# The sign of a weight's low word: one 32-bit VectorE instruction with two operands, or one 16-bit instruction with one

## The chip, the cores and the metric

The kernel runs on one core of one Trainium2 chip. The metric is the device time of one execution in microseconds (us). A core has five engines that work side by side, each through its own queue in order: TensorE (PE; its weight loads are PEld in the profile), VectorE (DVE), ScalarE (ACT), GpSimd (POOL) and SyncE (SP), which issues the transfers here.

## The reference

Three layers follow one another, all in float32:

```python
scores = scale * q @ k.T                     # 4 batches, 8 heads, 576 positions, 64 per head
attn   = (scores * Dmat) @ v                 # Dmat[i, j] = gamma[h] ** (i - j) for i >= j, else 0
x = attn, heads side by side                 # 2304 tokens x 512
h = x @ w_in                                 # 512 x 2048
y = (h * tanh(log1p(exp(h)))) @ w_out        # 2048 x 512
# then a routed layer: every token goes to one of 8 experts by sorted logits,
# 288 tokens each, out = relu(y @ w1[e]) @ w2[e]
```

The change lies in how `w_in` and `w_out` are prepared for the second layer.

## The kernel before

Matrix products are made from two words of each number: a high word (`hi`, the rounded value) and a low word (`lo`, the rest). A product is then three matmuls: high by high, low by high, high by low. So each weight tile of 128 x 512 has to be split once into `hi` and `lo`. There are 32 such tiles, 16 of `w_in` (`winh`, `winl`) and 16 of `w_out` (`woh`, `wol`). The host hands them over as 64-bit integers, so no plain float view of them is loaded: it is the kernel that turns the 64-bit element into a float32 one. `raw` is the loaded tile; `w0` is the low and `w1` the high 32-bit word of each element.

The class `convert` does that for one tile, in seven instructions:

- `c` (L160, ScalarE): copies `w1` with a scale into the work tile `t` (named y or spare in the profile).
- `x1` (L163, ScalarE): takes the 16-bit upper half of `w0` (`top`), and writes its top bits, as an integer, over `w0`, as 32-bit elements.
- `x` (L167, VectorE): takes the sign bit of `w1` and ors it into `w0`.
- `a` (L172, VectorE): shifts `t` left by three bits and ors `w0` into it. `t` is then the float32 weight. After it the next tile's transfer into the free buffer is issued (`fetch`, L141).
- `h` (L178, ScalarE): writes the high word. `l` (L181, GpSimd, in a few early cases VectorE): subtracts it from `t`, which gives the low word.

The second layer is laid out as a list of steps (`steps`, from `plan`). A step takes one block of 256 tokens and one of 16 slices of the hidden size: `ff_h` (L323, TensorE, 12 matmuls), the activation (`ff_a1` with L332 to L340, `ff_a2` with the reciprocal at L345, `ff_b1` L350, `ff_b2` L358, `ff_b3` L364 and L365), and three steps later `ff_y` (L417, six matmuls). The loop at L538 writes each engine's queue by hand. As long as there are weights left to convert, nearly every step (`CONV`) also converts one tile, and the attention of later blocks is spread over the steps by tables (`EARLY`, `MID`, `FOUR`).

In a step that converts, the queues hold, in this order:

- VectorE: `x`, `a`, L350 of the step before, L340, L365 of two steps before, L345, L358 of the step before.
- ScalarE: `x1` and `c` (both issued at the end of the step before), L332, L333, L334, L364 of two steps before, `h`.
- GpSimd: `l` of the step before, then the attention's multiplications (L232, L237) where there are any.

Four conversions come before the loop. The last of the 32 ends near 136 us; from then on the steps hold no conversion, and the rest of the time goes to the remaining steps of the second layer and to the routed layer.

Of the kernel before, what the change touches and what calls it, by code (L numbers as in the profile page):

```python
# [13 lines left out]
U16 = mybir.dt.uint16  # L14
I64 = mybir.dt.int64
AF = mybir.ActivationFunctionType
ALU = mybir.AluOpType
# [64 lines left out]
def first_part(ctx, tc, att, att_ht, att_hn, dtab, qtab, ktab, stab, wi, wo, wgb, ydram, L, constants, cst, begin, grid):  # L82
    nc = tc.nc
# [47 lines left out]
    raws = []  # L131
# [3 lines left out]
    done = [0]  # L135
# [7 lines left out]
    class convert:  # L143
# [3 lines left out]
        def __init__(self):  # L147
            _, self.hi, self.lo = parts[done[0]]
            w = raws[done[0]].bitcast(U32).rearrange("p (n two) -> p n two", two=2)
            self.w0, self.w1 = w[:, :, 0], w[:, :, 1]  # L150
            self.top = raws[done[0]].bitcast(U16).rearrange("p (n four) -> p n four", four=4)[:, :, 1]
            self.i = done[0]
            done[0] += 1

# [5 lines left out]
            nc.scalar.activation(self.t, self.w1.bitcast(F32), AF.Copy, scale=2.0 ** -112)  # L160

        def x1(self):
            nc.scalar.activation(self.w0, self.top, AF.Copy, scale=2.0 ** -13, bias=-0.4999)  # L163

        def x(self):
            w0 = self.w0
            nc.vector.scalar_tensor_tensor(w0, self.w1, 0x80000000, w0, op0=ALU.bitwise_and,  # L167
                                           op1=ALU.bitwise_or)

        def a(self):  # L170
            t = self.t.bitcast(U32)
# [364 lines left out]
    for x in slots.get(-1, []):  # L536
        x()
    for i in range(len(steps) + YL):  # L538
# [15 lines left out]
        if new:  # L554
            n, f = steps[i]
            alone = bool(now or old)
            eng = nc.vector if alone else nc.gpsimd
            if not alone:
                for x in slots.get(i, []):
                    x()  # L560
            if i and steps[i - 1] in inv:
                ff_b1(*steps[i - 1], nc.vector)
            ff_a1(n, f, i, alone)
            if i > 1:
                ff_b3(*steps[i - 2], eng)
            if now:
                now.h()
            if alone:
                for x in slots.get(i, []):
                    x()  # L570
                ff_h(*steps[i + 1], i + 1)
            while behind:
                behind.pop()()
            ff_a2(n, f)
            if i:
                ff_b2(*steps[i - 1])
            if eng is not nc.vector:
                ff_b1(n, f, nc.vector if i == len(steps) - 1 else eng)
# [979 lines left out]
```

## Time and profile before

| | |
|---|---|
| median of 3 runs | 824.83 us (824.33 to 826.1) |
| time of the profiled execution | 824.72 us |
| its span | 822.9 us |
| busy over the span: PE, DVE, ACT, POOL | 769.8, 532.7, 434.0, 472.4 us |
| instructions at the changed lines | 32 at L163, 32 at L167 |
| busy time of L167 | 24.2 us, 758 ns each |
| busy time of L163 | 21.3 us, 667 ns each |

The span runs from the first to the last recorded instruction; the execution's time is 1.8 us longer. Busy time is the time in which an engine worked on some instruction. Instructions of one engine overlap a little at their ends, so the distance from one start to the next is shorter than the duration where nothing has to be waited for. The chain of waits follows the work that ended last back to what released it. A row of a timeline gives the start, the duration, the engine, the line, the operation, the tile written and read, and in brackets the idle time before it and what ended it.

### The profile page before, as it was taken

Reading aid. Unit: us, or ns where it says so; the run is one execution under the profiler, and the core shown is the slowest. Engines: PE = TensorE matmul, PEld = TensorE weight load, DVE = VectorE, ACT = ScalarE, POOL = GpSimd, SP = SyncE. Lnnn points to the kernel's source line nnn. Section 1 sums busy time; section 2 is a strip of 40 time slices with the busy share of each in tenths; the row PEclk is TensorE's granted clock in tenths of the full one; section 3 lists DMA queues with packets and bytes.
Section 4 is the critical chain, followed back from the end, with each engine's and each line's share of the span. In section 5 each row is a group of like instructions: output and inputs, shape, how many; then the busy total and the mean of one; then the engine's idle time right before and its main releaser. Section 6 shows DMA issues by size and latency. Waiting matters only on the chain.

```text
span 822.9 us, 16272 instructions
## 1 busy us (share of the span) xinstructions
PE 769.8 (94%) x6151; PEld 704.5 (86%) x6151; DVE 532.7 (65%) x1262; ACT 434.0 (53%) x943; POOL 472.4 (57%) x539
## 2 busy tenths in 40 slices
PE   7698899999999999999999999749999999999993
PEld 6587777988998888888888999649899999999992
DVE  4999998646545887887879965676566563342110
ACT  3789998554545455455454555223544453564420
POOL 2643333645546666766666755115977985887811
PEclk8999999999999999999999999859999999999997
DMA  9646442011241201112100000063555764655301
GB/s 344 201 139 229 155 140 75 26 53 31 73 154 53 77 27 52 53 53 77 52 27 2 1 26 2 27 233 109 175 176 165 217 188 133 212 155 178 108 29 33
DMA packets 27322, 87.64 MB, mean 107 GB/s; under 512 B 4449, under 2 KB 5601, under 8 KB 27105
## 3 DMA queue, kind: packets, MB, share of 16 engines
q1 hardware_dynamic: 24160, 77.06, 28.6%
q0 software_dynamic: 3072, 9.44, 3.5%
q8 instruction: 50, 0.82, 0.4%
q14 instruction: 40, 0.32, 0.1%
HBM read 77.05 MB, written 9.44 MB: 105 GB/s over the span
## 4 chain that ended last, share of the span: by engine, by line
PE 71%; DVE 15%; issue 6%; POOL 3%; ACT 2%; DMA 2%; SPq 0%; DVEq 0%; POOLq 0%; ACTq 0%
PE ph L323 20%; PE hp L1273 9%; PE b_E L417 9%; PE op L1287 9%; PE b_F L417 8%; DVE rs L345 3%; DVE raw L167 2%; DVE y L172 2%; PE cnt L988 2%; PE b_A L223 2%; POOL wxl L827 1%; DVE hot L884 1%; DVE u L350 1%; PE b_E L453 1%; PE b_D L252 1%
## 5 line engine op out<-in xcount | busy, mean ns | idle before, releaser
L323 PE MATMUL ph<-xh,winh 128*128 128x256 f32 x576 | 164.8, 286 | 11.7 <-ACT d L332 6.8
L323 PE MATMUL ph<-xl,winh 128*128 128x256 f32 x576 | 161.5, 280 | 0.0
L323 PE MATMUL ph<-xh,winl 128*128 128x256 f32 x576 | 161.3, 280 | 0.0
L827 POOL TENSOR_TENSOR wxl<-wraw,wxh 128x1024 fp32r<-128x1024 f32 x60 | 142.3, 2395 | 29.4 <-ACT wxh L825 29.1
L365 POOL TENSOR_TENSOR gl<-u,gh 128x256 fp32r<-128x256 f32 x114 | 85.9, 754 | 91.6 <-ACT gh L364 90.8
L323 PEld LDWEIGHTS ph<-xh,winh 128*128 128x128 f32 x576 | 108.8, 189 | 25.6 <-ACT d L332 11.2
L332 ACT ACTIVATE d<-ph 128x256 f32<-128x256 f32 x144 | 54.9, 381 | 134.2 <-PE ph L323 119.0
L323 PEld LDWEIGHTS ph<-xh,winl 128*128 128x128 f32 x576 | 109.3, 190 | 4.2
L345 DVE RECIPROCAL u<-u 128x128 f32<-128x128 f32 x113 | 107.7, 953 | 3.9
L323 PEld LDWEIGHTS ph<-xl,winh 128*128 128x128 f32 x576 | 109.4, 190 | 0.5 <-DVE xl L259 0.3
L340 DVE TENSOR_TENSOR u<-d 128x128 f32<-128x128 f32 x113 | 41.5, 367 | 68.8 <-ACT d L334 62.6
L352 POOL TENSOR_TENSOR u<-d,u 128x128 f32<-128x128 f32 x112 | 52.4, 468 | 49.6 <-DVE u L345 49.6
L825 ACT ACTIVATE wxh<-wraw 128x1024 fp32r<-128x1024 f32 x64 | 67.3, 1052 | 18.8 <-DMA wraw<-in_wx_dram 18.8
L333 ACT ACTIVATE d<-d,half_b 128x256 f32<-128x256 f32 x144 | 73.5, 510 | 4.7
L353 POOL TENSOR_TENSOR u<-d,u 128x128 f32<-128x128 f32 x112 | 68.0, 607 | 8.8
L334 ACT ACTIVATE d<-d 128x256 f32<-128x256 f32 x144 | 60.2, 418 | 4.6
L364 ACT ACTIVATE gh<-u 128x256 fp32r<-128x256 f32 x144 | 57.9, 402 | 2.4 <-DVE u L358 2.2
L374 DVE SCALAR_TENSOR_TENSOR scr<-y,WG 128x512 bf16<-128x512 f32 x64 | 56.5, 883 | 0.4
L1264 DVE SCALAR_TENSOR_TENSOR htl<-hp,hth 128x288 fp32r<-128x288 f32 x64 | 28.4, 454 | 40.3 <-ACT hth L1276 39.8
L1276 ACT ACTIVATE hth<-hp 128x288 fp32r<-128x288 f32 x64 | 26.2, 409 | 51.8 <-PE hp L1273 51.3
L358 DVE SCALAR_TENSOR_TENSOR u<-u,ph 128x256 f32<-128x256 f32 x144 | 52.1, 362 | 0.0
L1273 PE MATMUL hp<-xth,wxh 128*128 128x288 f32 x256 | 50.1, 308 | 0.9 <-DVE htl L1264 0.9
(277 smaller groups left out, 1882.0 us busy)
## 6 DMA issues: line engine op xcount, KB each, us to landing
wraw<-in_wx_dram SPq DMA_DIRECT2D x64, 512.0 KB, 4.4
att<-in_att_dram SPq DMA_DIRECT2D x32, 512.0 KB, 5.0
raw<-in_wi_dram SPq DMA_DIRECT2D x16, 512.0 KB, 3.8
raw<-in_wo_dram SPq DMA_DIRECT2D x16, 512.0 KB, 3.5
ydram<-y SPq DMA_DIRECT2D x9, 512.0 KB, 2.8
WG<-in_wgb_dram SPq DMA_DIRECT2D x1, 2048.0 KB, 8.1
att<-in_att_ht_dram SPq DMA_DIRECT2D x4, 256.0 KB, 3.9
att<-in_att_hn_dram SPq DMA_DIRECT2D x4, 256.0 KB, 4.0
```

The source lines that it names most:

```text
L323: nc.tensor.matmul(ph, w[f][:, kt, :], x[:, kt, :], start=(k == 0), stop=(k == 11))
L333: nc.scalar.activation(df, df, AF.Square, bias=half_b, scale=-0.5)
L334: nc.scalar.activation(df, df, AF.Copy, bias=0.5, scale=0.5)
L345: nc.vector.reciprocal(r, r)
L353: eng.tensor_mul(u[:, 0, :], d[:, 1, :], r)
L364: nc.scalar.activation(gh, g, AF.Copy)
L365: eng.tensor_sub(gl, g, gh.bitcast(F32))
L417: nc.tensor.matmul(py[n][t], g[:, t * P:(t + 1) * P], w[f], start=(f == 0 and w is woh and g is gh), stop=(f == NF - 1 and g is gl))
L825: nc.scalar.activation(hi, raw, AF.Copy)
L827: rest = lambda eng: eng.tensor_sub(lo, raw, hi.bitcast(F32))
L1273: nc.tensor.matmul(hp, W[kt][w][:, s], x[:, kt, :], start=(k == 0), stop=(k == 11))
L1287: nc.tensor.matmul(op, W[4 + ft // 2][w][:, s], h[:, ft, :], start=(k == 0), stop=(k == 23))
```

## The change

`x1` writes the top bits as 16-bit integers, into the lower half of `w0` alone (element 0 of four 16-bit ones). `x` masks the sign out of the upper half of `w1` (element 3) and writes it to the upper half of `w0` (element 1). Together the two halves are the same 32-bit `w0` that `a` reads. `x` has one tensor operand and a constant now, and 16-bit elements with a step of four; it writes the half that `x1` reads, so it still comes after `x1`. `c`, `a`, `h`, `l` and the order of all queues stay as they are.

```diff
-            self.top = raws[done[0]].bitcast(U16).rearrange("p (n four) -> p n four", four=4)[:, :, 1]
+            self.q = raws[done[0]].bitcast(U16).rearrange("p (n four) -> p n four", four=4)
...
         def x1(self):
-            nc.scalar.activation(self.w0, self.top, AF.Copy, scale=2.0 ** -13, bias=-0.4999)
+            nc.scalar.activation(self.q[:, :, 0], self.q[:, :, 1], AF.Copy, scale=2.0 ** -13, bias=-0.4999)
 
         def x(self):
-            w0 = self.w0
-            nc.vector.scalar_tensor_tensor(w0, self.w1, 0x80000000, w0, op0=ALU.bitwise_and,
-                                           op1=ALU.bitwise_or)
+            nc.vector.tensor_scalar(self.q[:, :, 1], self.q[:, :, 3], 0x8000, None, op0=ALU.bitwise_and)
```

## Rows read from the trace of the kernel before

**Rows 1.** The page's span in 40 slices: busy tenths of an engine in each.
```profile
PE   7698899999999999999999999749999999999993
...
DVE  4999998646545887887879965676566563342110
```
**Rows 2.** Busy time by stretch; columns PE, PEld, DVE, ACT, POOL (instructions), clock, DMA share, GB/s.
```profile
20.00:40.00 20.00, 13.80 (x158) 12.21 (x157) 18.27 (x30) 14.62 (x33) 11.81 (x10) 1.00 0.60 201
40.00:45.00 5.00, 4.56 (x18) 3.84 (x18) 3.54 (x7) 3.77 (x11) 1.23 (x1) 0.66 0.31 103
45.00:70.00 25.00, 25.00 (x254) 21.74 (x252) 23.83 (x47) 20.80 (x50) 12.34 (x10) 1.00 0.54 186
70.00:105.00 35.00, 30.26 (x181) 24.38 (x180) 33.95 (x73) 33.63 (x73) 12.91 (x10) 1.00 0.52 178
```
**Rows 3.** The chain that ended last: start, length in us, engine and line.
```profile
84.51 0.61 DVE raw L167
...
134.42 1.66 PE ph L323 x12
```
**Rows 4.** Timeline of VectorE, one step: start, duration, engine, line, operation, tiles, shapes.
```profile
84.15 0.36 DVE L358 SCALAR_TENSOR_TENSOR u<-u,ph 128x256 f32<-128x256 f32 x1
84.43 0.68 DVE L167 SCALAR_TENSOR_TENSOR raw<-raw 128x512 uint32<-128x512 uint32 x1
85.21 0.69 DVE L172 SCALAR_TENSOR_TENSOR y<-y,raw 128x512 uint32<-128x512 uint32 x1
```
**Rows 5.** Timeline of ScalarE: one h, and L332 at the ends of stretches.
```profile
70.73 0.40 ACT L332 ACTIVATE d<-ph 128x256 f32<-128x256 f32 x1
...
73.97 0.36 ACT L332 ACTIVATE d<-ph 128x256 f32<-128x256 f32 x1
...
85.94 0.63 ACT L178 ACTIVATE winh<-y 128x512 fp32r<-128x512 f32 x1
...
104.64 0.36 ACT L332 ACTIVATE d<-ph 128x256 f32<-128x256 f32 x1
...
110.20 0.39 ACT L332 ACTIVATE d<-ph 128x256 f32<-128x256 f32 x1 [0.16 <-PE ph L323]
...
134.04 0.36 ACT L332 ACTIVATE d<-ph 128x256 f32<-128x256 f32 x1
```
**Rows 6.** Timeline of TensorE: two of its waits.
```profile
40.42 0.49 PE L323 MATMUL ph<-xh,winh 128*128 128x256 f32 x1 [2.13 <-ACT xh L258]
...
71.19 0.39 PE L323 MATMUL ph<-xh,winh 128*128 128x256 f32 x1 [1.17 <-ACT d L332]
```
**Rows 7.** Timeline of VectorE: three earlier x.
```profile
20.10 1.20 DVE L167 SCALAR_TENSOR_TENSOR raw<-raw 128x512 uint32<-128x512 uint32 x1
...
37.74 0.68 DVE L167 SCALAR_TENSOR_TENSOR raw<-raw 128x512 uint32<-128x512 uint32 x1
...
61.64 1.73 DVE L167 SCALAR_TENSOR_TENSOR raw<-raw 128x512 uint32<-128x512 uint32 x1
```
**Rows 8.** Timeline of GpSimd: two subtractions of l.
```profile
61.52 1.31 POOL L181 TENSOR_TENSOR wol<-y,woh 128x512 fp32r<-128x512 f32 x1
...
83.25 1.29 POOL L181 TENSOR_TENSOR wol<-y,woh 128x512 fp32r<-128x512 f32 x1 [2.12 <-ACT woh L178]
```
**Rows 9.** Groups by line and shape: busy us, mean ns of one, idle before.
```profile
L167 DVE SCALAR_TENSOR_TENSOR raw<-raw 128x512 uint32<-128x512 uint32 x32 | 24.2, 758 | 0.0
L172 DVE SCALAR_TENSOR_TENSOR y<-y,raw 128x512 uint32<-128x512 uint32 x30 | 23.0, 766 | 3.0
...
L350 DVE TENSOR_TENSOR u<-d,rs 128x256 f32<-128x256 f32 x31 | 13.0, 418 | 0.0
...
L389 DVE COPY yT<-b_C 128x512 f32<-128x512 f32 x3 | 2.0, 681 | 0.0
```
**Rows 10.** Groups by line and shape, ScalarE.
```profile
L163 ACT ACTIVATE raw<-raw 128x512 uint32<-128x512 uint16 x32 | 21.3, 667 | 0.0
```
**Rows 11.** The transfers of raw (L141), 78 to 135 us.
```profile
DMA to landing us min/median/max: 3.1/3.2/4.0
```

## The prediction, made before the changed kernel was run

> **What bounds the kernel now.** I read the page's slices first, to see where VectorE can matter at all. VectorE is busy nine tenths or more from about 21 to 124 us, and TensorE is short of that in just these slices; from the eighth slice on TensorE is nearly always full [rows 1]. All 32 conversions lie before 136 us, so only that part can become shorter, and what it becomes shorter by should reach the end unchanged, since behind it TensorE sets the pace.
>
> Next, the stretches. From 70 to 105 us VectorE is busy 33.95 of 35.00 us, ScalarE 33.63, TensorE 30.26. So VectorE is the limit there, but ScalarE stands 1% behind it. From 45 to 70 us TensorE is busy all 25.00 of 25.00 us: it is the limit there, whatever VectorE does. From 20 to 40 us VectorE is ahead again, 18.27 against ScalarE's 14.62 [rows 2].
>
> Third, the chain of waits: x (L167) stands on it in nearly every step up to 134.42 us, where TensorE takes over with its 12 matmuls of one step [rows 3].
>
> Fourth, the timelines. In a step VectorE does x from 84.43 us, a from 85.21, and so on through L358, seven instructions, without a pause. x itself lasts 0.68 us, and takes 0.78 from its own start to the start of a, since a reads what x wrote and starts 0.10 us after it has ended [rows 4]. ScalarE's h starts at 85.94, 0.04 us after a ended at 85.90: h is waiting for a, every step [rows 4, 5]. The steps from L332 at 73.97 to L332 at 104.64 are nine, 3.41 us each; the seven from 110.20 to 134.04 are 3.41 too. One step shows what ScalarE needs when nothing holds it up: from 70.73 to 73.97, 3.24 us [rows 5].
>
> TensorE has two long waits in the early part: it starts at 40.42 after 2.13 us without work, for an attention result that ScalarE copied behind its h, and then at 71.19 after 1.17 us for L332 [rows 6].
>
> **The change, part by part.**
>
> *x, the new price.* The old one has two SBUF operands of 512 elements. The new one has one operand and a constant, 512 elements of 16 bits. No row of before shows such an instruction. From above: a copy with one input of the same count, out of PSUM, takes 0.681 us, as long as the two-operand form does undisturbed [rows 9]. From below: an instruction that goes through half as many elements takes 0.418 [rows 9]. The low end holds if VectorE reads two elements of one operand in the time in which it read one of each of two; the high end holds if it goes element by element. I take the low end, 0.42: that two operands of 512 and one of 512 out of PSUM take the same shows that the engine reads two SBUF elements a cycle for the old x, and the new x needs only half of that. The copy out of PSUM is nearer in count, but not in where its operand lies. A gain below 0.42 would change nothing below, as will be seen.
>
> The Trainium skill has this price: VectorE: DVE Perf Modes, What auto-detection actually checks, lets a single-source instruction take two elements a cycle when source and destination are in SBUF and the outermost count is even, at any element size. With that page's fixed part of some 150 cycles, an estimate is 406 cycles at 0.96 GHz, 0.42 us; the sum would be the same. No run here shows it.
>
> *Steady steps.* With 0.42 in place of 0.68, x's place in VectorE's step falls from 0.78 to 0.52, and the step from 3.41 to 3.15. ScalarE needs 3.24. So ScalarE becomes the limit, and a step gains 3.41 - 3.24 = 0.17, not 0.26. Any x of 0.51 or less gives that same gain. Nine steps give 1.5 us, seven more 1.2, together 2.7. The step at 70.73 is at 3.24 already, and those between 104.64 and 110.20 have TensorE as a limit (the L332 at 110.20 waits for it [rows 5]): nothing from these.
>
> *The early x.* At 20.10 and at 61.64 x lasts 1.20 and 1.73 us [rows 7]. At 61.64 the subtraction l of GpSimd runs from 61.52 to 62.83 [rows 8], and x ends at 63.37, 0.54 us after it: x sat still until GpSimd was done and then went through its 512 elements. With half the cycles I take 0.27 off behind such a wait. At 20.10 that moves h, L332 and all that follows: -0.27. Three more x, up to 48 us, are followed by an a that is itself held by GpSimd (a lasts 0.766 on average against 0.69 undisturbed [rows 4, 9]); what x gains there a waits longer: 0. The x at 37.74 is undisturbed, and a, h and the copy that TensorE waits for until 40.42 follow: -0.26 [rows 6, 7]. So TensorE starts there 0.53 earlier. From 45 to 70 us it is full, so the x in between bring it nothing; but the x at 61.64 sits behind GpSimd, whose work there follows TensorE's, so that its wait ends 0.53 earlier and it takes 0.27 less: L332 at 70.73 comes 0.8 earlier.
>
> Here a rule speaks against the change. The two-operand x waits for GpSimd in these rows. By the Trainium skill, SBUF — State Buffer, Who interferes with whom, a VectorE instruction with one SBUF operand at one element a cycle never meets GpSimd, but in a mode that reads two it blocks and is blocked for the whole instruction. The trace agrees as far as the two-operand form goes (the 0.54 us above). By that rule the faster x keeps the waits and the slower one loses them.
>
> *The new phase against GpSimd.* In the steady steps l runs from 83.25 to 84.54, and x really starts at 84.51, when L358 ends [rows 4, 8]. When h no longer waits for a, x reaches VectorE up to 0.3 us before l is over. If it has to wait, the loop is: 0.27 for x, 0.10 to a, a 0.69, 0.04 to h, h 0.63, 0.09 to l, l 1.29, together 3.11, below 3.24. So this wait costs nothing; it would from 0.13 us on.
>
> *x1.* It reads what it read, and writes 16 bits where it wrote 32. Its 0.667 [rows 10] I take as unchanged. No ScalarE row of before writes 16-bit elements, so it could be dearer; that is a rival below. It gains nothing: it still goes through 512 elements.
>
> *What is late next.* Conversions come every 3.24 us in place of 3.41. The transfer of the next tile but one leaves when a ends and is there 3.2 us later (4.0 at most) [rows 11]; x1 needs it one ScalarE step and one h after that, 3.24 + 0.5 = 3.8. That cover holds but for the slowest transfer, which would cost 0.2 once. TensorE has 30.26 us of work in 35.00 [rows 2] and would have 33.3 us for it: not the limit.
>
> *Sum.* 0.8 + 2.7 = 3.5 us off the profiled execution's 824.72 us (822.9 of span and 1.8 around it; the median of the runs is 0.1 above it): 821.2 us.
>
> **Rivals.**
>
> 1. *x keeps one element a cycle*, so the change doesn't do what its halves suggest. For it: the copy at 0.681. Then x's place stays at 0.78 and the steady steps stay at 3.41. What is left is that x, with one operand, no longer sits behind GpSimd: all x together are 32 x (0.758 - 0.68) = 2.5 us above the undisturbed one [rows 9]; behind most of these a has to wait for the same GpSimd instruction, so I give half, 1.3 us: 823.4. If x's end comes 0.09 sooner as well, the 16 steady steps give 1.4 more: 822.0.
>
> 2. *Writing 16 bits costs ScalarE more* (slower). The place is x1. ScalarE has only 3.41 - 3.24 = 0.17 us of room in a step, and is the new limit. If x1 grows by less than 0.17, part of the gain goes; from there on each step gets longer than before. If writing halves of words made it go over its elements twice, at most 0.667 more, the step is 3.91, 0.50 longer, 16 steps 8.0: with the early gain of 0.8 the time is about 832; at half of that growth about 826.5. Against it: x1 reads 16-bit elements with the same step already, at 0.667 beside the 0.63 of h on 512 elements of 32 bits [rows 5, 10].
>
> 3. *The clock comes back.* From 40 to 45 us the granted clock is 0.66 on average (so partly at 1.2 in place of 2.4 GHz), behind the wait of 2.13 us; the stretches beside it show 1.00 [rows 2, 6]. If the shorter wait keeps it at 2.4 GHz, 5 x 0.34 = 1.7 us of TensorE's time comes back in a stretch where it is the limit: 819.5. Against it: 0.26 of 2.13 us is little.
>
> 4. *Nothing arrives*: TensorE's work or something else between takes the 0.17 of each step, and the time stays within 0.5 us: 824.5. Against it: TensorE's idle time in these steps, 4.7 us in 35.
>
> **Chances.** The forecast 0.55, its own range 820.4 to 822.4 (without the early part 822.0; with a ScalarE step of 3.21, 820.7). Rival 1 0.17, rival 2 0.11, rival 3 0.08, rival 4 0.09. A range for 8 in 10 goes from a little below rival 3 to just short of rival 4's value: 819.3 to 824.4. A difference under 0.2%, 1.65 us, can't be told from none, so faster is below 823.2: the forecast, rival 3 and two thirds of rival 1, 0.75; within: the rest of rival 1, rival 4 and a mild rival 2, 0.16; slower, the rest of rival 2: 0.09.
>
> **What would show it.** Right: x near 0.42 us and followed by a 0.10 later; L332 to L332 near 3.24 us from 74 to 104 and from 110 on; ScalarE busier than VectorE in those stretches, with h right behind L364 and not behind a; the last L332 of a converting step near 130.5 in place of 134.04; x1 at 0.667. Wrong: x at 0.68 (rival 1), x1 above 0.83 (rival 2), a clock of 1.00 from 40 to 45 (rival 3), TensorE without idle time between 74 and 104 at steps of 3.4 (rival 4).

## The result, and the profile after

The changed kernel takes 832.1 us (831.37 to 833.24, 4 runs) against 824.58 us for the kernel before: a ratio of 1.0092 (95% interval 1.007 to 1.0113). The profiled execution's span grew from 822.9 to 831.5 us. The forecast was 821.2 us, in a range up to 824.4: wrong, and on the wrong side. Rival 2 (x1 dearer, so that ScalarE's longer step decides) is what happened; that its 832 us is met is partly luck, as the part on the prediction shows.

The price of the two changed instructions is the first thing to look up, for all instances of x1 (L163) and of x (L166): the count, and the shortest, middle and longest duration in ns.

```profile
L163 ACT ACTIVATE raw<-raw x32: 1336/1360/1387, 10.7 to 140.6; 128x512 uint16<-128x512 uint16 x32
...
L166 DVE TENSOR_SCALAR raw<-raw x32: 731/749/1524, 12.0 to 142.0; 128x512 uint16<-128x512 uint16 x32
```

x1 takes 1.36 us where it took 0.667 [rows 10], in all 32 cases. x was to take 0.42 and takes 0.75, more than the 0.68 of the instruction it replaces [rows 4].

The stretch that answers to the last of [rows 2] (PE, PEld, DVE, ACT, POOL, clock, DMA share, GB/s):

```profile
70.00:105.00 35.00, 27.11 (x165) 22.27 (x165) 31.92 (x65) 34.42 (x67) 10.90 (x10) 1.00 0.47 160
```

VectorE has fallen from 33.95 to 31.92 us of work in the 35, and ScalarE has risen from 33.63 to 34.42: ScalarE is the limit now, and VectorE and TensorE do less because they wait for it. The ScalarE timeline of one step shows how:

```profile
85.21 0.62 ACT L176 ACTIVATE woh<-y 128x512 fp32r<-128x512 f32 x1
85.73 1.34 ACT L163 ACTIVATE raw<-raw 128x512 uint16<-128x512 uint16 x1
86.81 0.70 ACT L160 ACTIVATE y<-raw 128x512 f32<-128x512 f32 x1
87.40 0.38 ACT L330 ACTIVATE d<-ph 128x256 f32<-128x256 f32 x1
...
88.69 0.40 ACT L362 ACTIVATE gh<-u 128x256 fp32r<-128x256 f32 x1
89.00 0.61 ACT L176 ACTIVATE winh<-y 128x512 fp32r<-128x512 f32 x1
```

It is back to back (the two instructions left out as well, L331 and L332): from h at 85.21 to h at 89.00 are 3.79 us without a pause, and h no longer waits for a. From x1's start to c's start are 1.08 us, where before they were 0.55. VectorE and TensorE in the same step:

```profile
87.11 0.74 DVE L166 TENSOR_SCALAR raw<-raw 128x512 uint16<-128x512 uint16 x1 [0.20 <-ACT raw L163]
```

```profile
87.84 0.39 PE L321 MATMUL ph<-xh,winh 128*128 128x256 f32 x1 [1.66 <-ACT d L330]
```

x now waits 0.20 us for x1, and TensorE waits 1.66 us for ScalarE in every second step. The first activation of a step (L332 before, L330 now) stands at these places at the ends of the two steady stretches:

```profile
76.04 0.37 ACT L330 ACTIVATE d<-ph 128x256 f32<-128x256 f32 x1
...
110.22 0.36 ACT L330 ACTIVATE d<-ph 128x256 f32<-128x256 f32 x1
...
115.67 0.36 ACT L330 ACTIVATE d<-ph 128x256 f32<-128x256 f32 x1
...
142.30 0.36 ACT L330 ACTIVATE d<-ph 128x256 f32<-128x256 f32 x1
```

Nine steps take 34.18 us (before 30.67 [rows 5]) and seven take 26.63 (before 23.84): 3.80 a step against 3.41, 6.3 us for the 16. The last one is 8.3 us late (142.30 against 134.04): besides the 6.3, 2.1 us came before the first of them, and 0.1 was won back between the two stretches. In the chain of waits from 78 to 92 us only ScalarE's lines are left, x1 with 39% of it, and 15% for which the view names no wait; x is gone from it.

### The profile page after: what moved, and what is told of

Same layout as the page of the kernel before. It is cut to its first block, busy times and chain, and to the rows that moved or that the text cites. A ratio compares the mean times of both kernels' runs of the same rounds, so it can differ in the third digit from the quotient of the medians.

```text
span 831.5 us, 16272 instructions
## 1 busy us (share of the span) xinstructions
PE 767.2 (92%) x6151; PEld 702.2 (84%) x6151; DVE 538.1 (65%) x1262; ACT 450.8 (54%) x943; POOL 472.5 (57%) x539
## 4 chain that ended last, share of the span: by engine, by line
PE 70%; ACT 11%; DVE 8%; issue 6%; POOL 2%; DMA 1%; POOLq 0%; DVEq 0%; ACTq 0%
PE ph L321 19%; PE hp L1271 9%; PE b_E L415 8%; PE op L1285 8%; PE b_F L415 8%; ACT raw L163 4%; PE cnt L986 2%; PE b_A L221 2%; ACT d L331 1%; ACT y L160 1%; DVE hot L882 1%; PE b_E L451 1%; PE b_D L250 1%; PE b_F L451 1%; POOL wxl L825 1%
## 5 line engine op out<-in xcount | busy, mean ns | idle before, releaser
L330 ACT ACTIVATE d<-ph 128x256 f32<-128x256 f32 x144 | 55.2, 383 | 131.4 <-PE ph L321 115.5
L331 ACT ACTIVATE d<-d,half_b 128x256 f32<-128x256 f32 x144 | 73.7, 512 | 4.7
L332 ACT ACTIVATE d<-d 128x256 f32<-128x256 f32 x144 | 60.5, 420 | 4.5
```

The costliest lines, as they stand in the source:

```text
L331: nc.scalar.activation(df, df, AF.Square, bias=half_b, scale=-0.5)
L332: nc.scalar.activation(df, df, AF.Copy, bias=0.5, scale=0.5)
```

## Experiments

Theory A: ScalarE's x1 is the whole loss; it takes twice as long, because it writes 16-bit elements with gaps between them, and ScalarE is the limit. Theory B: the new x carries much of it.

**x alone.** The kernel after, with x1 writing 32-bit elements as before.

```diff
-            nc.scalar.activation(self.q[:, :, 0], self.q[:, :, 1], AF.Copy, scale=2.0 ** -13, bias=-0.4999)
+            nc.scalar.activation(self.w0, self.q[:, :, 1], AF.Copy, scale=2.0 ** -13, bias=-0.4999)
```

> x1 writes 32-bit elements again as before; only x is the new 16-bit instruction with one operand. Theory A (x1's 16-bit write is the whole loss: ScalarE 1.36 in place of 0.67 us): x1 is back at 0.67, ScalarE needs 3.24 us a step again, VectorE's step is 3.41 + 0.08 for the longer x (0.75 against 0.68), so steps of 3.49 and 16 x 0.08 = 1.3 us: about 826 us, 0.2% over before. Theory B (the new x carries much of the loss: it is longer, it waits for x1 and it keeps waiting for GpSimd): x1 at 0.67, but steps of 3.6 or more and 828 us or more.

Measured: 826.91 us, ratio to before 1.0024 (1.0013 to 1.0036). x1 is back at 0.663 us. VectorE's timeline of one step:

```profile
86.92 0.75 DVE L166 TENSOR_SCALAR raw<-raw 128x512 uint16<-128x512 uint16 x1
...
90.40 0.74 DVE L166 TENSOR_SCALAR raw<-raw 128x512 uint16<-128x512 uint16 x1
```

From x to x are 3.48 us: VectorE is the limit again, 0.07 us slower than before, since x's place grew from 0.78 to 0.85. So what x1 writes carries 5.2 of the 7.5 us: theory A in the main, but not the whole of the loss. The new x is a small loss, not a gain. Its 0.07 us make 1.1 us over 16 steps; where the rest of the 2.25 us between the medians (826.91 and 824.66) lies is not shown. In the profiled execution the kernel is even with the one before when the conversions are over (the first activation at 142.91 us against 143.00), because it came to the steady steps 1.2 us ahead (72.80 against 73.97).

**c twice.** The kernel before, with nothing narrow in it, but one more pass over 512 elements on ScalarE.

```diff
             nc.scalar.activation(self.t, self.w1.bitcast(F32), AF.Copy, scale=2.0 ** -112)
+            nc.scalar.activation(self.t, self.w1.bitcast(F32), AF.Copy, scale=2.0 ** -112)
```

> The kernel before with c issued twice on ScalarE, nothing narrow anywhere: it adds a second 512-element pass of some 0.55 us to ScalarE in each conversion, about what x1 grew by (its place in the queue went from 0.56 to 1.10 us). Theory A: ScalarE's step is 3.24 + 0.55 = 3.79, steps of 3.8 us as in the changed kernel, and the time comes within 1 us of its 832. Theory B: ScalarE's time explains less than half, so about 827.

Measured: 836.11 us, ratio 1.0142 (1.0123 to 1.0161). That ScalarE's time alone is enough is clear, but the size is missed by 4 us. ScalarE's timeline:

```profile
130.15 0.66 ACT L160 ACTIVATE y<-raw 128x512 f32<-128x512 f32 x1
130.84 0.69 ACT L161 ACTIVATE y<-raw 128x512 f32<-128x512 f32 x1
131.41 0.39 ACT L333 ACTIVATE d<-ph 128x256 f32<-128x256 f32 x1
```

The second c writes what the first wrote and starts only when that one has ended, 0.69 us after its start and not 0.55. Steps are 3.92 us (from 127.47 to 131.41 one of 3.94), which makes 2 of the 4 us over 16 steps. Three of the stretches of 10 us between 80 and 130 us have a granted clock of 0.83 or 0.84, so partly 1.2 in place of 2.4 GHz. Where the other 2 us lie is left open: the profiled executions of the two kernels are only 0.8 us apart (spans of 832.3 and 831.5), so their traces don't show it.

**Forms.** The kernel before, with single instructions on a spare tile ahead of everything.

> The kernel before with 9 ScalarE and 9 VectorE instructions on a spare tile ahead of everything, when GpSimd and the transfers stand still; only their durations are read. Old x1 (32-bit out, step of two) 0.67; new x1 (16-bit out, step of four) 1.36 if the write itself is slow, 0.67 if it was the other engines' traffic. If the step makes it slow: 1.36 for every 16-bit output with gaps (step of four and of two, in the word that is read or another), 0.67 for a dense 16-bit output. If the type makes it slow: 1.36 for the dense one too. If reading and writing the same word makes it slow: only the first is 1.36. VectorE: old x 0.69, new x 0.75; the one-operand form on 32-bit elements is 0.42 or less if it takes two elements a cycle, 0.68 if one; a 16-bit output with gaps above its dense form if the partial write is what costs.

Only the durations are read, from one execution, so there is no interval (the time of the whole, 835.31 us, says nothing here, since the kernel starts later). ScalarE, in this order: old x1; new x1; the same into another word; 16-bit out, 4 bytes apart; 16-bit dense; 16-bit, 8 bytes apart from a dense input; 32-bit dense; 16-bit, 8 bytes apart from a dense float32 input; 16-bit dense from float32.

```profile
2.60 0.67 ACT L132 ACTIVATE fa<-fa 128x512 uint32<-128x512 uint16 x1 [0.55 <-POOL fa L122]
3.30 1.35 ACT L132 ACTIVATE fa<-fa 128x512 uint16<-128x512 uint16 x1
4.39 1.44 ACT L132 ACTIVATE fa<-fa 128x512 uint16<-128x512 uint16 x1
5.55 0.87 ACT L132 ACTIVATE fa<-fa 128x512 uint16<-128x512 uint16 x1
6.45 0.67 ACT L132 ACTIVATE fa<-fa 128x512 uint16<-128x512 uint16 x1
7.16 1.38 ACT L132 ACTIVATE fa<-fa 128x512 uint16<-128x512 uint16 x1
8.56 0.68 ACT L132 ACTIVATE fa<-fa 128x512 uint32<-128x512 uint16 x1
9.27 1.34 ACT L132 ACTIVATE fa<-fa 128x512 uint16<-128x512 f32 x1
10.64 0.63 ACT L132 ACTIVATE fa<-fa 128x512 uint16<-128x512 f32 x1
```

This tells the causes apart. It is not the type (dense 16-bit 0.63 to 0.67), not the word being read and written at once (the other word is 1.44), not the input (dense or not, 16-bit or float32, 1.34 to 1.38), and not the work of VectorE or GpSimd beside it. These were not idle as planned: GpSimd still wrote to SBUF until 4.76 us, VectorE went through its own series from 4.34 to 9.16, and TensorE worked from 4.82 to 9.37. But the old x1 took its 0.67 beside GpSimd's write, and the row at 9.27 took 1.34 when VectorE and GpSimd had ended and the transfers had hardly begun (a share of 0.13 from 9.20 to 10.60). What is left is the gaps in the output. VectorE, one operand each but the first: old x; new x; 32-bit 8 bytes apart; 32-bit dense out; 16-bit dense out; then 16-bit 8 bytes apart from a dense input, 16-bit 4 bytes apart, all 16-bit dense, all 32-bit dense.

```profile
4.34 0.69 DVE L144 SCALAR_TENSOR_TENSOR fb<-fb 128x512 uint32<-128x512 uint32 x1 [4.34 <-POOL fb L122]
5.07 0.76 DVE L145 TENSOR_SCALAR fb<-fb 128x512 uint16<-128x512 uint16 x1
5.86 0.43 DVE L145 TENSOR_SCALAR fb<-fb 128x512 uint32<-128x512 uint32 x1
6.20 0.42 DVE L145 TENSOR_SCALAR fb<-fb 128x512 uint32<-128x512 uint32 x1
6.65 0.43 DVE L145 TENSOR_SCALAR fb<-fb 128x512 uint16<-128x512 uint16 x1
7.12 0.76 DVE L145 TENSOR_SCALAR fb<-fb 128x512 uint16<-128x512 uint16 x1
7.91 0.46 DVE L145 TENSOR_SCALAR fb<-fb 128x512 uint16<-128x512 uint16 x1
8.40 0.29 DVE L145 TENSOR_SCALAR fb<-fb 128x512 uint16<-128x512 uint16 x1
8.73 0.43 DVE L145 TENSOR_SCALAR fb<-fb 128x512 uint32<-128x512 uint32 x1
```

So the low end of the prediction, 0.42, is the price of one operand, but not of this output: in 16-bit elements 8 bytes apart it is 0.76, 4 bytes apart 0.46.

**Both halves 4 bytes apart.** If the distance is the cause, the same change with another layout should not lose. The work tile t is dense, so its halves are 4 bytes apart; c scales the high word in place, and a takes it from there.

```diff
-            nc.scalar.activation(self.t, self.w1.bitcast(F32), AF.Copy, scale=2.0 ** -112)
+            nc.scalar.activation(self.w1.bitcast(F32), self.w1.bitcast(F32), AF.Copy, scale=2.0 ** -112)
...
-            nc.scalar.activation(self.q[:, :, 0], self.q[:, :, 1], ...
+            nc.scalar.activation(self.r[:, :, 0], self.q[:, :, 1], ...      # r: t as pairs of 16 bits
...
-            nc.vector.tensor_scalar(self.q[:, :, 1], self.q[:, :, 3], ...
+            nc.vector.tensor_scalar(self.r[:, :, 1], self.q[:, :, 3], ...
...
-            nc.vector.scalar_tensor_tensor(t, t, 3, self.w0, ...
+            nc.vector.scalar_tensor_tensor(self.z, self.w1, 3, self.z, ...  # z: t as 32-bit words
```

> The changed kernel with both 16-bit halves written into the work tile t, where a 32-bit word follows the last at 4 bytes and not at 8; c scales the high word in place and a reads it from there. Theory A, made sharper by the forms (a 16-bit write costs by its distance: alone 0.87 us at 4 bytes and 1.35 at 8 on ScalarE, 0.46 and 0.76 on VectorE): x1 0.87, ScalarE's step 3.24 + 0.20 = 3.44, VectorE's 3.41 - 0.78 + 0.56 = 3.19, so steps of 3.44 and about 824.5 us, no difference from before that can be measured. Rival (it is the two engines' 16-bit writes beside each other, or a read and a write of the same words): x1 stays above 1.1 and the steps at 3.7 or more: 829 or more.

Measured: 819.14 us against 823.16 for the kernel before on that chip, ratio 0.9952 (0.9931 to 0.9972). The rival is out. x1 and x:

```profile
L162 ACT ACTIVATE y<-raw x30: 761/782/822, 10.5 to 126.8; 128x512 uint16<-128x512 uint16 x30
...
L165 DVE TENSOR_SCALAR y<-raw x30: 439/460/789, 11.3 to 128.1; 128x512 uint16<-128x512 uint16 x30
```

x1 is 0.78, not the 0.87 that I had counted with, and an undisturbed step is 3.28 us (from 105 us on, 3.27 to 3.32), not 3.44. The kernel is 4.0 us faster than before, where no difference was expected, and the steps explain little of that. Two of the first nine take 3.92 and 3.83 us, since x1 waits 0.56 and 0.46 us for its tile, so these nine (from 69.07 to 99.81 us) are 3.42 us on average, as before. Of the 6.1 us by which the last converting step comes earlier (127.95 against 134.04), 4.9 are there at the first steady step (69.07 against 73.97). The profiled execution is the fastest of the seven, with a granted clock of 1.00 from 10 to 20 us where the one before had 0.82 and 0.50; how much of the 4.9 us is due to the layout is not shown.

**x1 wide and dense.** The same, but x1 writes 32-bit words into t, and only x writes halves.

```diff
-            nc.scalar.activation(self.r[:, :, 0], self.q[:, :, 1], ...
+            nc.scalar.activation(self.z, self.q[:, :, 1], ...
```

> As the run beside it, but x1 writes dense 32-bit elements into t (alone 0.68 us), and only x writes 16-bit halves, 4 bytes apart (alone 0.46 us). Theory A: ScalarE's step 3.24 and VectorE's 3.19, steps of 3.24 us, and what the prediction gave the change comes true here: about 821.2 us, 0.4% under before. Rival (the faster x only waits, for GpSimd's subtraction or for c, behind which it now stands): steps of 3.35 or more, 823.5 or more.

Measured: 819.02 us against 823.16, ratio 0.9943 (0.9923 to 0.9962). The two engines in one step:

```profile
87.19 0.62 ACT L174 ACTIVATE woh<-y 128x512 fp32r<-128x512 f32 x1
87.71 0.66 ACT L162 ACTIVATE y<-raw 128x512 uint32<-128x512 uint16 x1
...
90.39 0.61 ACT L174 ACTIVATE winh<-y 128x512 fp32r<-128x512 f32 x1
```

```profile
85.76 0.56 DVE L165 TENSOR_SCALAR y<-raw 128x512 uint16<-128x512 uint16 x1
...
88.98 0.52 DVE L165 TENSOR_SCALAR y<-raw 128x512 uint16<-128x512 uint16 x1
```

A step is 3.20 us, ScalarE back to back and VectorE at the same pace, so the rival is out. This is the step that the prediction gave the change, reached by another layout (with c in place and a reading the scaled word from there), and the interval of the gain, 0.57% (0.38 to 0.77), holds the 0.43% forecast. In this execution the clock of the early part is nearly as before (0.84 and 0.50 from 10 to 20 us, 0.66 from 40 to 45), so the two can be set side by side: the first steady step comes 1.7 us earlier (72.24 against 73.97), the 16 steps, two of them with a wait for a tile, take 2.2 us less, 0.4 come between the two stretches, and the last converting step is 4.3 us earlier (129.74 against 134.04). These two versions beat both kernels; they can't be told from each other.

**Forms, once more.** Which distance costs what.

> The kernel before with 7 ScalarE and 7 VectorE instructions on spare tiles ahead of everything, 512 elements each with a dense 32-bit input (VectorE: 16-bit halves at 4 bytes for its 16-bit outputs); only the durations are read. Outputs in this order: 16-bit at 4, 8 and 16 bytes, 32-bit at 8 and 16 bytes, 16-bit dense, 32-bit dense. If the cost of a 16-bit write grows with the distance: ScalarE 0.87, 1.35, above 2; if it stops at a pass of its own for each element: 0.87, 1.35, 1.35. 32-bit at 8 bytes 0.67; at 16 bytes 0.67 if only 16-bit writes pay, 1.3 if half of a row of bytes being skipped is what costs. VectorE: 0.46, 0.76, then 0.76 or 1.4; 32-bit 0.43.

ScalarE in the order of the expectation (again only durations are read; the whole took 833.21 us):

```profile
2.06 0.80 ACT L129 ACTIVATE fa<-dt 128x512 uint16<-128x512 f32 x1
2.88 1.34 ACT L129 ACTIVATE fa<-dt 128x512 uint16<-128x512 f32 x1
4.25 2.51 ACT L129 ACTIVATE fa<-dt 128x512 uint16<-128x512 f32 x1
6.80 0.66 ACT L129 ACTIVATE fa<-dt 128x512 uint32<-128x512 f32 x1
7.49 1.10 ACT L129 ACTIVATE fa<-dt 128x512 uint32<-128x512 f32 x1
8.62 0.63 ACT L129 ACTIVATE fa<-dt 128x512 uint16<-128x512 f32 x1
9.28 0.63 ACT L129 ACTIVATE fa<-dt 128x512 uint32<-128x512 f32 x1
```

The cost grows with the distance, for 32-bit outputs too, and it follows the step in elements of the output's own type more nearly than the bytes: a step of 2 costs 0.80 or 0.66 (16 or 32 bits), a step of 4 1.34 or 1.10, a step of 8 2.51. At the same 8 bytes the 32-bit output takes 0.03 us more than a dense one and the 16-bit output 0.71. On VectorE, 16-bit outputs took 0.43 dense, 0.74 at 8 and 1.32 at 16 bytes, 32-bit ones 0.43, 0.43 and 0.63. (Its first, at 4 bytes, began while GpSimd wrote SBUF, and its 0.74 is left out; the first series has 0.46.)

## Why the prediction was wrong, step by step

- *x1 is unchanged at 0.667.* This is the step that failed, and the one that decided. It took 1.36. The text looked at what x1 reads (16-bit elements, with gaps, at 0.667) and at how many elements there are; what it writes is what counted, as x alone shows: the same input with a 32-bit output is back at 0.663. Rival 2 named the place and the size ("made it go over its elements twice, at most 0.667 more") and got 0.11. Its picture of a second pass is not what the rows show in general: the time goes on growing with the step, to 2.51.
- *x at 0.42.* Wrong by 0.33 us, for the same reason: the output's gaps. The price of one operand was right: 0.43 for 512 elements of 32 bits, against 0.69 for the two-operand form. The Trainium skill's rule in VectorE: DVE Perf Modes, What auto-detection actually checks, is borne out by that row, at 0.43 against the estimate of 0.42 worked out from it; for 16-bit outputs 8 bytes apart, the measured 0.76 decides.
- *ScalarE is right behind VectorE.* Right, and the reason why the loss came through whole: with 0.17 us of room, x1's 0.54 us more in the queue (1.08 to 1.12 against 0.55 to 0.57, start to start) left a step of 3.24 + 0.54 = 3.78; measured 3.80. Rival 2's condition (above 0.17 each step gets longer) was met by far, and its 16 steps of 0.50 compare with 16 of 0.39. That the sum came to 832 all the same is luck: its steps were 1.7 us too long together, and the early part, which it let gain 0.8, lost 2.1.
- *The early part gains 0.8.* Wrong: by the first steady step the changed kernel was 2.1 us late. The loss came at the end of that part: at 56 us the two kernels were even (the first activation at 56.55 against 56.56), and the four steps to 76.04 lost the 2.1. It is x1's again: with its 32-bit output (x alone) the same four steps lost only 0.15. From 45 to 70 us TensorE was to be the limit whatever VectorE does, and that holds only as long as ScalarE has room: it has 22.23 us of work there in place of 20.80 [rows 2], and TensorE is no longer full. (It was not short in just those slices in which VectorE is full, either: in two of the five it stands at nine tenths as well [rows 1].)

```profile
45.00:70.00 25.00, 23.14 (x231) 20.32 (x232) 23.70 (x46) 22.23 (x47) 12.22 (x10) 1.00 0.56 178
```

- *x keeps waiting for GpSimd.* Right, though in the kernel after only one of 32 does so for long; in x alone it is five, with 0.95 to 1.78 us. In the kernel after, GpSimd's L235 and x:

```profile
32.48 1.04 POOL L235 TENSOR_TENSOR att<-att,kt 128x512 f32<-128x512 f32 x1
```

```profile
32.61 1.52 DVE L166 TENSOR_SCALAR raw<-raw 128x512 uint16<-128x512 uint16 x1 [0.38 <-ACT raw L163]
```

  x ends at 34.13, 0.61 us after GpSimd's 33.52, as the old x ended 0.54 after it [rows 7, 8]. That one operand meets GpSimd at all agrees with the Trainium skill, SBUF — State Buffer, Who interferes with whom, for a form that reads two elements a cycle.
- *The transfer of the next tile.* The cover was thinner than thought. In the version with steps of 3.20 us (x1 wide and dense) ScalarE's x1 waited for its tile twice, here 0.46 us, where 0.2 had been counted for once:

```profile
74.90 0.67 ACT L162 ACTIVATE y<-raw 128x512 uint32<-128x512 uint16 x1 [0.46 <-DMA raw<-in_wi_dram]
```

- *Rival 3, the clock.* Its sign came, not its time: from 40 to 45 us the granted clock was 1.00 in the kernel after, where it had been 0.66 [rows 2]. But the low stretches moved as a whole. From 10 to 20 us the clock was 1.00 where it had been 0.82 and 0.50, and from 30 to 40 it was 0.84 and 0.82 where it had been 1.00. Before and after, from 15 to 20 us:

```profile
15.00:20.00 5.00, 5.00 (x42) 4.52 (x41) 2.90 (x5) 2.80 (x6) 0.54 (x1) 0.50 1.02 410
```

```profile
15.00:20.00 5.00, 3.48 (x42) 2.90 (x43) 4.33 (x7) 4.39 (x7) 0.96 (x1) 1.00 1.01 397
```

  From the first activation at 37.20 us to the next at 43.35 the changed kernel went from 0.90 us behind to 0.33 ahead (36.30 and 43.68 before); by 56 us the two were even. What the clock is worth in the whole is not separated by any run.
- *ScalarE's step and the sum.* With x1's gaps gone and x's at 4 bytes, 3.20 us a step (3.24 forecast) and 0.57% less time. So the limit and the size were right for a kernel that this change was not. The terms fit less well than their sum: 2.2 us from the 16 steps, because of the waits for tiles (2.7 forecast), and 1.7 from the early part (0.8 forecast), in a version that also moves c and a.

## What to carry to other kernels

Price an instruction by its output's layout as well as by its input and count: on ScalarE an output with a step of four elements took 1.7 to 2.1 times as long as a dense one here, on VectorE 1.5 to 1.8 times. Where two engines are within 5% of each other in a step, an edit that relieves one has to be checked for what it does on the other, to the tenth of a us. Halves of words can be worth writing, but into a tile where they are neighbours.

## What the runs showed of the hardware that was not expected

- ScalarE, 512 elements from a dense float32 input: 0.63 us dense, 0.80 with a step of two, 1.34 of four, 2.51 of eight for 16-bit outputs; 0.63, 0.66 and 1.10 with a step of one, two and four for 32-bit ones. The Trainium skill has one element per cycle for every function and for two- and four-byte types alike (ScalarE: Activation LUTs, What ACT_TABLE_LOAD costs); these rows agree for dense outputs (0.63 for both types) and, within 0.03 us, for 32-bit ones with a step of two; with wider steps they do not. Why the gaps cost is not settled by these runs.
- VectorE with one operand: 0.43 us for 512 elements of 32 bits, dense or with a step of two, 0.63 with a step of four; 0.29 for dense 16-bit ones in and out; 0.46, 0.76 and 1.32 for 16-bit outputs with a step of two, four and eight. The input's gaps cost nothing with a 32-bit output (0.42 and 0.43 into a dense one); with a dense 16-bit output the step of four in the input made 0.43 of 0.29.
